# A fused attention and MoE kernel whose matmuls read the moving operand as two interleaved halves

## Chip, core and metric

The kernel runs on one NeuronCore of one Trainium2 chip, as one launch. The metric is the device time of that core in microseconds, taken as the median of three runs; lower is better. No other core works at the same time, and the profile shows the TensorE clock granted at its upper level, 2.4 GHz, through nearly the whole execution.

## What is computed

Four batches of 12480 tokens, 128 channels each, pass through two attentions with 32 inducing points. The 49920 results then pass through one two-layer network with a hidden width of 2048:

```python
h = mab(I, x)                 # 32 x 128 per batch
x = mab(x, h)                 # 12480 x 128 per batch: softmax over 32, times h
h = x @ w_in                  # 49920 x 2048
g = h * (1 / (1 + exp(-1.702 * h)))
out = g @ w_out               # 49920 x 128
```

## The kernel before

**Blocks and chunks.** The output is made in 98 blocks of tokens (list `work`): 96 of 512 tokens, and two of 384 that hold what is left over of two batches each. The hidden width is cut into 16 chunks of 128; two chunks make a step, so a block has 8 steps. Tokens always lie along the free dimension, channels or hidden units on the partitions, so the tokens are the moving operand of every product of the network.

**First products** (`firsts`, L527). A tile `st` holds the stacked softmax weights of a block, 512 tokens wide, and a tile `hw` the 32 rows of h times `w_in` in stacked form. Each chunk is one matmul of 512 columns; the two chunks of a step fill the two PSUM banks of a tile `ph`. There are two `ph` tiles.

**Activation and splitting.** ScalarE applies the activation from `ph` into a float32 tile `g` (`gelus`, L553). From step 12 on, `g` is split into a rounded part `hi` and a rest `lo`: `hi` comes either from ScalarE, a second activation from `ph` (L569), or from VectorE, a copy of `g` (L576), whichever engine `choose` finds less loaded; `lo` is always VectorE's subtraction (L585, `rests`).

**Second products** (`seconds`, L704 to L706). Each chunk adds three matmuls into one PSUM bank `pso`, because `w_out` is split as well: `wl` with `hi`, `wh` with `lo`, `wh` with `hi`. All of these operands are of type fp32r, and a matmul takes one column per clock. The first 24 chunk products (L690) use plain float32 `g` and `wf` instead; each is two matmul instructions, and an instruction takes two clocks per column. The last block is written in `ending` (L627 to L629): its last four chunks are done in halves of 256 columns, the right halves into a second bank `side`, so that most of the result is copied and sent while the right half is still being computed.

**Output.** When a block's 16 chunks are added up, `out` copies `pso` to a tile `ob` on ScalarE (L605) or VectorE (L608), and `store` sends it to `outT`. There are two `pso` banks and two `ob` tiles.

**Attention.** The attentions of batches 1 to 3 are worked in between: TensorE visits of 10 to 35 small matmuls each (L351 and L370 for the first attention, L993 and L359 for the second), with exponentials on ScalarE and transposes, maxima and subtractions on VectorE.

**Order of the work.** The order on each engine is fixed when the program is built. `Plan` is a list scheduler: each `Job` has an engine, an occupation in ns and a latency, and `Plan.step` takes the job that could begin first, by rank among equals. Where a job may go to ScalarE or VectorE, the one that would end first gets it. The occupation of a matmul of `w` columns is one of its costs:

```python
            one_ = 2.5 + 0.447 * tokens(i)
...
                occ = 3 * (2.5 + 0.447 * w)
```

Tiles `st`, `hw`, `hi` and `lo` come from `spaced`, which adds 16 elements to each tile's row; within a tile the 512 tokens of a chunk are one contiguous run of 2 KB per partition.

Of the kernel before, what the change touches and what calls it, by code (L numbers as in the profile page):

```python
# [17 lines left out]
P = 128  # L18
# [252 lines left out]
def on_act(n):  # L271
    return 70 + 0.833 * n, 215 + 0.833 * n


def on_dve(n):
    return 75 + 1.042 * n, 200 + 1.042 * n
# [7 lines left out]
def set_attention_then_moe(ctx: ExitStack, tc, xT, x, indT, w_in, w_out, outT):  # L284
    nc = tc.nc
    dve, act, pe_ = nc.vector, nc.scalar, nc.tensor
# [11 lines left out]
    t0 = 0  # L298
# [65 lines left out]
    def weigh(pa, s, aT, xn, i, n, second=None):  # L364
# [10 lines left out]
            i += 1  # L375
        return i

    def blocks(some):
        return sum(sups[s][2] // 32 for s in some)

    work = []
# [94 lines left out]
    phs, gs, his, los = [[Unit() for _ in range(n)] for _ in range(4)]  # L476
# [6 lines left out]
    def new_st(name):  # L483
        return Unit(NG, parts=G if len(name) == 3 else 2 * RG * G)
# [4 lines left out]
    def tokens(i):  # L489
        return sum(p[2] for p in work[steps[i][0]][1])  # L490

    def late(least, most):
        return lambda: most if ahead() >= AHEAD else least
# [16 lines left out]
    def firsts():  # L510
        for i in range(n):
            bi, k = steps[i]
            key, of = work[bi]
            if key not in st_units:
                st_units[key] = new_st(key)
            for b, _, _, _ in of:
                for c in range(G):
                    h_units.setdefault((b, c), Unit(uses_hw[b], parts=G))
            stu = st_units[key]
            hwu = [h_units[b, 2 * k // 4] for b, _, _, _ in of]  # L520

            def emit(i=i, k=k, of=of, stu=stu, hwu=hwu):
                st, ph = stu.ap, phs[i].ap
                for c in range(2):
                    ch = 2 * k + c
                    for (b, at, w, _), u in zip(of, hwu):
                        pe_.matmul(  # L527
                            ph[:, c, at:at + w], u.ap[:, ch % 4 * P:(ch % 4 + 1) * P],
                            st[:, at:at + w], start=True, stop=True,
                        )  # L530
                counts["F"] = i + 1

            one_ = 2.5 + 0.447 * tokens(i)
            yield Job("PE", emit, 2 * one_, 2 * one_ + 200, [stu, *hwu], takes=[(r_ph, phs[i])], rank=(1, i), slack=late(0, 800),
                gate=lambda: not plan.asked(r_ph),
            )
# [56 lines left out]
    def store(bi, ob):  # L593
        _, of = work[bi]
        for b, at, w, t0 in of:
            def emit(at=at, w=w, t0=t0):
                nc.sync.dma_start(outT[:, t0:t0 + w], ob.ap[:, at:at + w])
            yield Job("SP", emit, 430, 2500, [ob], rank=(3, bi), size=w * 512)

    def out(bi, pso):  # L600
        w = sum(p[2] for p in work[bi][1])
        ob = Unit(len(work[bi][1]))

        def by_act():
            act.copy(ob.ap[:, 0:w], pso.ap[:, 0:w])  # L605

        def by_dve():
            dve.tensor_copy(ob.ap[:, 0:w], pso.ap[:, 0:w])  # L608

        yield [  # L610
            Job("ACT", by_act, *on_act(w), [pso], [], [(r_ob, ob)], rank=(0, bi)),
            Job("DVE", by_dve, *on_dve(w), [pso], [], [(r_ob, ob)], rank=(0, bi)),
        ]
        yield from store(bi, ob)

    def ending(bi, i0):
        w = tokens(i0)
        h = w // 2
        b, at, _, t0 = work[bi][1][0]
        ps, side, kept = Unit(3, parts=NCH), Unit(1, parts=2 * ENDING), Unit(3)  # L620
        firsts_ = [(i, c) for i in range(i0, i0 + NG) for c in range(2)]
        split = firsts_[-2 * ENDING:]

        def three(o, i, c, cols, start, stop):
            ch = 2 * (i - i0) + c
            hi, lo = his[i].ap[:, c, cols], los[i].ap[:, c, cols]
            pe_.matmul(o, wl[:, ch, :], hi, start=start, stop=False)  # L627
            pe_.matmul(o, wh[:, ch, :], lo, start=False, stop=False)  # L628
            pe_.matmul(o, wh[:, ch, :], hi, start=False, stop=stop)  # L629

        def job(i, c, cols, right):
            n_ = cols.stop - cols.start
            first = (i, c) == (split[0] if right else firsts_[0])
            last = (i, c) == firsts_[-1]
            unit = side if right else ps

            def emit():
                three(unit.ap[:, 0:h] if right else unit.ap[:, cols], i, c, cols, first, last)
                counts["S"] += not right

            occ = 3 * (2.5 + 0.447 * n_)
            ch = 2 * (i - i0) + c
            return Job(
                "PE", emit, occ, occ + 200, [his[i], los[i], w_out_units[ch // G]], rank=(2, i),
                **({"takes": [(r_po, unit)]} if first else {"joins": [unit]}),
            )

        for i, c in firsts_:
            his[i].uses += (i, c) in split
            los[i].uses += (i, c) in split  # L650
            yield job(i, c, slice(0, h if (i, c) in split else w), False)

        def keep():
            act.copy(kept.ap[:, 0:w], ps.ap[:, 0:w])

        def add():
            dve.tensor_add(kept.ap[:, h:w], kept.ap[:, h:w], side.ap[:, 0:h])  # L657

        def send(cols):
            def emit():  # L660
                nc.sync.dma_start(outT[:, t0 + cols.start:t0 + cols.stop], kept.ap[:, cols])
            return emit

        done = Unit(1)
        plan.spawn(iter([
            Job("ACT", keep, *on_act(w), [ps], [], [(r_ob, kept)], rank=(0, bi)),
            Job("SP", send(slice(0, h)), 430, 2500, [kept], rank=(3, bi), size=h * 512),
            Job("DVE", add, *on_dve(h), [kept, side], [], joins=[done], rank=(0, bi)),
            Job("SP", send(slice(h, w)), 430, 2500, [done], rank=(3, bi), size=h * 512),
        ]))  # L670
        for i, c in split:
            yield job(i, c, slice(h, w), True)

    def seconds():
        psos = {}
        for i, (bi, k) in enumerate(steps):
            if bi == len(work) - 1:
                yield from ending(bi, i)
                return
            w = tokens(i)  # L680
            if k == 0:
                psos[bi] = Unit(parts=NCH)
            pso = psos[bi]
            for c in range(2):
                ch = 2 * k + c

                join = {"joins": [pso]} if ch else {"takes": [(r_po, pso)]}

                def whole(i=i, c=c, ch=ch, w=w, pso=pso):
                    pe_.matmul(  # L690
                        pso.ap[:, 0:w], wf[:, ch * P:(ch + 1) * P], gs[i].ap[:, c, 0:w],
                        start=(ch == 0), stop=(ch == NCH - 1),
                    )
                    counts["S"] += 1

                if i < plain:
                    occ = 4 * (1 + 0.4185 * w)
                    yield Job("PE", whole, occ, occ + 200, [gs[i], wf_units[ch // G]], rank=(2, i), **join)
                    continue

                def emit(i=i, c=c, ch=ch, w=w, pso=pso):
                    o = pso.ap[:, 0:w]
                    hi, lo = his[i].ap[:, c, 0:w], los[i].ap[:, c, 0:w]
                    pe_.matmul(o, wl[:, ch, :], hi, start=(ch == 0), stop=False)  # L704
                    pe_.matmul(o, wh[:, ch, :], lo, start=False, stop=False)  # L705
                    pe_.matmul(o, wh[:, ch, :], hi, start=False, stop=(ch == NCH - 1))  # L706
                    counts["S"] += 1

                occ = 3 * (2.5 + 0.447 * w)
                yield Job(  # L710
                    "PE", emit, occ, occ + 200, [his[i], los[i], w_out_units[ch // G]], rank=(2, i), **join,
                )
            if k == NG - 1:
                plan.spawn(out(bi, pso))
# [78 lines left out]
    def attention(b):  # L793
# [109 lines left out]
        pah = Unit(parts=len(WEIGH))  # L903
        i = 0
        total = blocks(range(NS))
        for v, some in enumerate(WEIGH):

# [432 lines left out]
    wf = const.tile([P, WHOLE * WC], F32, name="wf") if WHOLE else None  # L1340
# [483 lines left out]
    plan.spawn(fast([2, 3], False))  # L1824
    plan.spawn(to_gelu())
    plan.spawn(firsts())
    plan.spawn(attentions())
    plan.spawn(loads_xT())
# [15 lines left out]
    for thread in (gelus, rests, seconds, lay_out):  # L1844
        plan.spawn(thread())
# [34 lines left out]
```

## Time and profile before

| | us |
|---|---|
| median of 3 runs | 1568.87 |
| lowest, highest | 1568.35, 1569.07 |
| span of the profiled execution, first to last instruction | 1566.2 |
| TensorE (PE) matmul busy | 1559.7 |
| weight loads (PEld) busy | 1226.0 |
| VectorE (DVE) busy | 1340.9 |
| ScalarE (ACT) busy | 1321.2 |

The page gives the span of the profiled execution and no total time for it beside that. The median of the runs is 2.7 us above the span: that is taken here as what lies around it, the start ahead of the first instruction and the wait for the last store.

In the rows, a group is a source line, an engine, an operation, the tile written and the tiles read, the shape and a count; then the busy time in us and the mean duration of one in ns, and behind the second bar the idle time of the engine just before these instructions and what ended it. Matmuls are pipelined: a row's mean duration (393 ns) holds the time in the pipeline, and the pace is the distance from one start to the next.

### The profile page before, as it was taken

Reading aid. Unit: us, or ns where it says so; the run is one execution under the profiler, and the core shown is the slowest. Engines: PE = TensorE matmul, PEld = TensorE weight load, DVE = VectorE, ACT = ScalarE, POOL = GpSimd, SP = SyncE. Lnnn points to the kernel's source line nnn. Section 1 sums busy time; section 2 is a strip of 40 time slices with the busy share of each in tenths; the row PEclk is TensorE's granted clock in tenths of the full one; section 3 lists DMA queues with packets and bytes.
Section 4 is the critical chain, followed back from the end, with each engine's and each line's share of the span. In section 5 each row is a group of like instructions: output and inputs, shape, how many; then the busy total and the mean of one; then the engine's idle time right before and its main releaser. Section 6 shows DMA issues by size and latency. Waiting matters only on the chain. (4 is left out here: it accounts for less than half of the span.)

```text
span 1566.2 us, 21639 instructions
## 1 busy us (share of the span) xinstructions
PE 1559.7 (100%) x7707; PEld 1226.0 (78%) x7707; DVE 1340.9 (86%) x1641; ACT 1321.2 (84%) x1515; POOL 0.7 (0%) x6
## 2 busy tenths in 40 slices
PE   9999999999999999999999999999999999999999
PEld 7477878877877887887787887887788888888887
DVE  6999888888888888889889888988898888888886
ACT  6799888888887888888988888888888888888876
POOL 0000000000000000000000000000000000000000
PEclk9999999999999999999999999999999999999999
DMA  7455144161132404416014512512201111111100
GB/s 272 165 167 141 33 90 91 34 202 48 46 137 86 93 29 95 84 35 220 29 41 151 129 46 53 110 45 84 66 26 46 34 40 33 36 38 31 41 27 21
DMA packets 84617, 125.06 MB, mean 80 GB/s; under 512 B 12128, under 2 KB 51872, under 8 KB 79136
## 3 DMA queue, kind: packets, MB, share of 16 engines
q1 hardware_dynamic: 84512, 123.69, 28.4%
q8 instruction: 62, 1.02, 0.3%
q14 instruction: 43, 0.35, 0.1%
HBM read 70.43 MB, written 25.56 MB: 61 GB/s over the span
## 5 line engine op out<-in xcount | busy, mean ns | idle before, releaser
L585 DVE TENSOR_TENSOR lo<-g,hi 128x1024 fp32r<-128x1024 f32 (+1 forms) x772 | 929.4, 1215 | 164.5 <-ACT hi L569 150.4
L553 ACT ACTIVATE g<-ph 128x1024 f32<-128x1024 f32 (+1 forms) x784 | 805.1, 1032 | 205.7 <-PE ph L527 84.7
L704 PE MATMUL pso<-hi,wl 128*128 128x512 f32 (+1 forms) x1528 | 600.3, 393 | 0.0
L705 PE MATMUL pso<-lo,wh 128*128 128x512 f32 (+1 forms) x1528 | 599.4, 392 | 0.1
L706 PE MATMUL pso<-hi,wh 128*128 128x512 f32 (+1 forms) x1528 | 599.3, 392 | 0.0
L569 ACT ACTIVATE hi<-ph 128x1024 fp32r<-128x1024 f32 (+1 forms) x459 | 473.4, 1033 | 3.8 <-PE pso L706 3.8
L527 PE MATMUL ph<-st,hw 128*128 128x512 f32 x1536 | 457.6, 398 | 0.9 <-ACT g L553 0.9
L527 PEld LDWEIGHTS ph<-st,hw 128*128 128x128 f32 x1536 | 283.0, 188 | 85.2 <-ACT g L553 10.7
L705 PEld LDWEIGHTS pso<-lo,wh 128*128 128x128 f32 x1528 | 287.0, 188 | 66.2 <-DVE lo L585 1.0
L704 PEld LDWEIGHTS pso<-hi,wl 128*128 128x128 f32 x1528 | 287.0, 188 | 65.5 <-issue 0.2
L706 PEld LDWEIGHTS pso<-hi,wh 128*128 128x128 f32 x1528 | 287.0, 188 | 65.2
L576 DVE CAST hi<-g 128x1024 fp32r<-128x1024 f32 (+1 forms) x313 | 211.1, 681 | 27.2 <-ACT g L553 23.4
L605 ACT COPY ob<-pso 128x512 f32<-128x512 f32 (+1 forms) x76 | 45.8, 603 | 6.7 <-PE pso L706 6.7
L690 PE MATMUL pso<-g,wf 128*128 128x512 f32 x48 | 23.2, 598 | 0.1
L351 PE MATMUL pa<-xt,indT_sb 128*32 128x512 f32 x160 | 19.9, 598 | 0.0
L608 DVE COPY ob<-pso 128x512 f32<-128x512 f32 x21 | 14.3, 681 | 4.9 <-PE pso L706 4.8
L370 PEld LDWEIGHTS pa<-xn,t 128*32 128x32 f32 x576 | 15.2, 110 | 3.3 <-issue 2.9
L370 PE MATMUL pa<-xn,t 128*32 128x128 f32 x576 | 17.6, 274 | 0.0
L1133 DVE TENSOR_TENSOR t<-t,two 128x512 f32<-128x512 f32 (+1 forms) x27 | 16.8, 621 | 0.8 <-ACT two L1122 0.2
L1117 DVE STREAM_TRANSPOSE t<-e 128x512 f32<-128x512 f32 x23 | 16.2, 704 | 0.0
L1112 DVE TENSOR_TENSOR e<-e,sm 128x512 f32<-128x512 f32 x23 | 15.6, 680 | 0.0
L1100 DVE TENSOR_REDUCE sm<-e 128x16 f32<-128x512 f32 x23 | 15.6, 678 | 0.0
(203 smaller groups left out, 477.0 us busy)
## 6 DMA issues: line engine op xcount, KB each, us to landing
xt<-in_xT SPq DMA_DIRECT2D x42, 1024.0 KB, 7.1
out_T<-ob SPq DMA_DIRECT2D x95, 256.0 KB, 2.0
xn<-in_x SPq DMA_DIRECT2D x72, 256.0 KB, 6.3
st<-two SPq DMA_DIRECT2D x184, 64.0 KB, 2.0
st<-t SPq DMA_DIRECT2D x184, 64.0 KB, 2.0
hw<-t SPq DMA_DIRECT2D x48, 64.0 KB, 2.8
raw<-in_w_in SPq DMA_DIRECT2D x4, 512.0 KB, 8.7
raw<-in_w_out SPq DMA_DIRECT2D x4, 512.0 KB, 5.0
```

Of the source, the lines that this page charges most:

```text
L351: pe_.matmul(pa[32 * j:32 * j + 32, 0:w], indT_sb, xg[:, j], start=True, stop=True)
L370: pe_.matmul(pa[32 * j:32 * j + 32, 0:P], aT[0:q, kk, :], xn[0:q, kk] if second is None or kk < BLK // 2 else second[0:q, kk - BLK // 2], ...
L527: pe_.matmul(ph[:, c, at:at + w], u.ap[:, ch % 4 * P:(ch % 4 + 1) * P], st[:, at:at + w], start=True, stop=True,)
L553: act.activation(gs[i].ap[:, :, 0:w], phs[i].ap[:, :, 0:w], AF.Gelu_apprx_sigmoid)
L569: act.activation(his[i].ap[:, :, 0:w], phs[i].ap[:, :, 0:w], AF.Gelu_apprx_sigmoid)
L576: dve.tensor_copy(his[i].ap[:, :, 0:w], gs[i].ap[:, :, 0:w])
L585: dve.tensor_sub(los[i].ap[:, :, 0:w], gs[i].ap[:, :, 0:w], his[i].ap[:, :, 0:w].bitcast(F32))
L605: act.copy(ob.ap[:, 0:w], pso.ap[:, 0:w])
L690: pe_.matmul(pso.ap[:, 0:w], wf[:, ch * P:(ch + 1) * P], gs[i].ap[:, c, 0:w], start=(ch == 0), stop=(ch == NCH - 1),)
L704: pe_.matmul(o, wl[:, ch, :], hi, start=(ch == 0), stop=False)
L705: pe_.matmul(o, wh[:, ch, :], lo, start=False, stop=False)
L706: pe_.matmul(o, wh[:, ch, :], hi, start=False, stop=(ch == NCH - 1))
```

## The change

Every matmul of the network reads its moving operand through `woven`: the free dimension is seen as two halves, and columns are taken from the two halves in turns. For a 512-column matmul of 4-byte elements the halves begin 1 KB apart; column 0 is token 0, column 1 token 256, column 2 token 1, and so on. The product's columns in PSUM come out in that order. The activation and the split keep the order they find. The second product weaves once more, so that a block's result has its tokens permuted twice, and the copy from PSUM to `ob` (or, for the last block, `keep`, `add` and `send`) puts them back: it reads PSUM with a step of four elements and writes four runs. The last block's first products are read straight; its second products are woven, and its two stores write runs of 128 tokens to `outT`. In the 384-column blocks the first products weave each batch's 192 columns by themselves. Attention's matmuls are not changed. In the planner the price per column goes from 0.447 to 0.417 ns.

```diff
+    def woven(t):
+        return t.rearrange("p (a b) -> p b a", a=2)
+
+    def unwoven(t, parts):
+        order = "p (c a s) -> p a s c" if parts == 1 else "p (c a s) -> p s a c"
+        return t.rearrange(order, a=2, s=2)
+
+    def runs(t):
+        return t.rearrange("p (s a c) -> p s a c", a=2, s=2)
...
-                            st[:, at:at + w], start=True, stop=True,
+                            order(st[:, at:at + w]), start=True, stop=True,
...
-            one_ = 2.5 + 0.447 * tokens(i)
+            one_ = 2.5 + 0.417 * tokens(i)
...
-            act.copy(ob.ap[:, 0:w], pso.ap[:, 0:w])
+            act.copy(runs(ob.ap[:, 0:w]), unwoven(pso.ap[:, 0:w], len(work[bi][1])))
...
-            dve.tensor_copy(ob.ap[:, 0:w], pso.ap[:, 0:w])
+            dve.tensor_copy(runs(ob.ap[:, 0:w]), unwoven(pso.ap[:, 0:w], len(work[bi][1])))
...
-            hi, lo = his[i].ap[:, c, cols], los[i].ap[:, c, cols]
+            half = slice(cols.start // 2, cols.stop // 2)
+            hi, lo = woven(his[i].ap[:, c, 0:w])[:, half], woven(los[i].ap[:, c, 0:w])[:, half]
...
         def keep():
-            act.copy(kept.ap[:, 0:w], ps.ap[:, 0:w])
+            act.copy(
+                kept.ap[:, 0:w].rearrange("p (q s b) -> p q s b", q=2, s=2),
+                ps.ap[:, 0:w].rearrange("p (q b s) -> p q s b", q=2, s=2),
+            )
 
         def add():
-            dve.tensor_add(kept.ap[:, h:w], kept.ap[:, h:w], side.ap[:, 0:h])
+            right = kept.ap[:, h:w].rearrange("p (s b) -> p s b", s=2)
+            dve.tensor_add(right, right, side.ap[:, 0:h].rearrange("p (b s) -> p s b", s=2))
...
-                nc.sync.dma_start(outT[:, t0 + cols.start:t0 + cols.stop], kept.ap[:, cols])
+                nc.sync.dma_start(
+                    outT[:, t0:t0 + w].rearrange("p (s q b) -> p q s b", q=2, s=2)[:, q],
+                    kept.ap[:, cols].rearrange("p (s b) -> p s b", s=2),
+                )
...
-                    hi, lo = his[i].ap[:, c, 0:w], los[i].ap[:, c, 0:w]
+                    hi, lo = woven(his[i].ap[:, c, 0:w]), woven(los[i].ap[:, c, 0:w])
```

The L690 matmuls and the prices of the second products change in the same way. The number of instructions is the same on TensorE (7021 in the program's order, 7707 in the trace, where a float32 matmul stands more than once) and on SyncE (686). Because of the new price the planner orders them otherwise. On ScalarE the activations into `hi` go from 459 to 471, the copies to `ob` from 76 to 64, the casts L1122 from 17 to 12 and the copies L821 from 14 to 13; on VectorE the casts into `hi` go from 313 to 301, the copies to `ob` from 21 to 33, the casts L1125 from 10 to 15 and the copies L824 from 7 to 8. Lines behind the new helpers are 10 to 20 higher in the changed kernel.

On VectorE, early in the program where batch 1's first attention is being worked in, the order before has one copy of a block's result among the subtractions `lo`:

```order
L585 TENSOR_TENSOR lo<-g,hi 128x1024
L608 COPY ob<-pso 128x512
L1133 TENSOR_TENSOR t<-t,two 128x512
L832 TENSOR_REDUCE mx<-e 128x1
L824 COPY e<-pa 128x512
L832 TENSOR_REDUCE mx<-e 128x1
L576 CAST hi<-g 128x1024
```

and the order of the changed kernel at about the same place:

```order
L595 TENSOR_TENSOR lo<-g,hi 128x1024
L618 COPY ob<-pso 128x512
L595 TENSOR_TENSOR lo<-g,hi 128x1024 x2
L1153 TENSOR_TENSOR t<-t,two 128x512
L586 CAST hi<-g 128x1024 x2
L595 TENSOR_TENSOR lo<-g,hi 128x1024
L852 TENSOR_REDUCE mx<-e 128x1 x2
L852 TENSOR_REDUCE mx<-e_last 64x1
L595 TENSOR_TENSOR lo<-g,hi 128x1024
L586 CAST hi<-g 128x1024
L595 TENSOR_TENSOR lo<-g,hi 128x1024 x4
L618 COPY ob<-pso 128x512
```

The copy of `e` from PSUM and the attention's maxima have moved back behind more subtractions, and the next block's copy has come to VectorE too.

On TensorE, batch 1's second visit of the first attention's products (L370) stands between first and second products of the network. Before:

```order
L704 MATMUL pso<-hi,wl 128x512
L705 MATMUL pso<-lo,wh 128x512
L706 MATMUL pso<-hi,wh 128x512
L370 MATMUL pa<-xn,t 32x128 x32
L527 MATMUL ph<-st,hw 128x512 x4
L704 MATMUL pso<-hi,wl 128x512
```

and in the changed kernel:

```order
L724 MATMUL pso<-hi,wl 128x512
L725 MATMUL pso<-lo,wh 128x512
L726 MATMUL pso<-hi,wh 128x512
L537 MATMUL ph<-st,hw 128x512 x2
L370 MATMUL pa<-xn,t 32x128 x32
L537 MATMUL ph<-st,hw 128x512 x2
```

The visit now splits the two steps of first products, and stands some 50 rows later in TensorE's order (row 720 for row 671).

## Rows read from the trace of the kernel before

**Rows 1.** The page: engines' busy time, share of the span, instructions.
```profile
PE 1559.7 (100%) x7707; PEld 1226.0 (78%) x7707; DVE 1340.9 (86%) x1641; ACT 1321.2 (84%) x1515; POOL 0.7 (0%) x6
```

**Rows 2.** Matmuls by line and shape.
```profile
L704 PE MATMUL pso<-hi,wl 128*128 128x512 f32 x1496 | 589.5, 394 | 0.0
L705 PE MATMUL pso<-lo,wh 128*128 128x512 f32 x1496 | 588.6, 393 | 0.1
L706 PE MATMUL pso<-hi,wh 128*128 128x512 f32 x1496 | 588.5, 393 | 0.0
L527 PE MATMUL ph<-st,hw 128*128 128x512 f32 x1536 | 457.6, 398 | 0.9 <-ACT g L553 0.9
L690 PE MATMUL pso<-g,wf 128*128 128x512 f32 x48 | 23.2, 598 | 0.1
...
L704 PE MATMUL pso<-hi,wl 128*128 128x384 f32 x32 | 10.8, 338 | 0.0
...
L627 PE MATMUL pso<-hi,wl 128*128 128x512 f32 x12 | 4.7, 394 | 0.0
```

**Rows 3.** Timeline, last block: start us, us; 21 starts apart; no DVE, ACT after 1558.61.
```profile
1555.17 0.39 PE L627 MATMUL pso<-hi,wl 128*128 128x512 f32 x1
...
1556.34 1.02 ACT L569 ACTIVATE hi<-ph 128x1024 fp32r<-128x1024 f32 x1
...
1557.39 1.22 DVE L585 TENSOR_TENSOR lo<-g,hi 128x1024 fp32r<-128x1024 f32 x1 [0.59 <-ACT hi L569]
...
1558.65 0.40 PE L627 MATMUL pso<-hi,wl 128*128 128x512 f32 x1
...
1560.04 0.28 PE L627 MATMUL pso<-hi,wl 128*128 128x256 f32 x1
```

**Rows 4.** Timeline of TensorE at 63.5 us: six float32 matmuls in a row.
```profile
63.52 2.74 PE L690 MATMUL pso<-g,wf 128*128 128x512 f32 x6
```

**Rows 5.** Stretches: us, PE, PEld, DVE, ACT, POOL busy (instructions), PEclk, DMA share, GB/s.
```profile
60.00:160.00 100.00, 100.00 (x451) 70.14 (x450) 91.30 (x122) 87.96 (x103) 0.00 (x0) 1.00 0.56 171
760.00:860.00 100.00, 100.00 (x458) 77.40 (x458) 89.36 (x100) 85.06 (x95) 0.00 (x0) 1.00 0.23 78
1260.00:1360.00 100.00, 100.00 (x434) 80.95 (x433) 85.64 (x92) 85.10 (x94) 0.00 (x0) 1.00 0.12 35
```

**Rows 6.** Waits: who waited for whom, us in total, times, longest us.
```profile
DVE lo L585 <- ACT hi L569: 150.4, 236, 1.8
ACT g L553 <- PE ph L527: 84.7, 113, 3.7
...
PEld ph L527 <- ACT g L553: 10.7, 31, 0.8
```

**Rows 7.** Copies of the result, contiguous, and reads with a step beside contiguous ones.
```profile
L605 ACT COPY ob<-pso 128x512 f32<-128x512 f32 x74 | 44.8, 606 | 5.8 <-PE pso L706 5.8
L608 DVE COPY ob<-pso 128x512 f32<-128x512 f32 x21 | 14.3, 681 | 4.9 <-PE pso L706 4.8
...
L1049 ACT ACTIVATE e<-e 128x512 f32<-128x512 f32 x23 | 12.8, 620 | 0.1
L832 DVE TENSOR_REDUCE mx<-e 128x1 f32<-128x512 f32 x18 | 11.9, 675 | 0.1
...
L1288 ACT ACTIVATE sq<-raw 128x512 f32<-128x512 f32 x8 | 5.5, 689 | 0.0
...
L944 DVE TENSOR_REDUCE all_h<-t 32x128 f32<-32x512 f32 x3 | 3.2, 1071 | 0.0
```

**Rows 8.** Timeline of the end.
```profile
1561.64 0.58 ACT L654 COPY ob<-pso 128x512 f32<-128x512 f32 x1 [4.28 <-PE pso L629]
...
1562.25 1.65 SPq L661 DMA_DIRECT2D out_T<-ob  x2
...
1562.74 0.28 PE L629 MATMUL pso<-hi,wh 128*128 128x256 f32 x1
1563.12 0.42 DVE L657 TENSOR_TENSOR ob<-ob,pso 128x256 f32<-128x256 f32 x1 [4.50 <-PE pso L629]
```

More of the change, by code (lines that the diff above doesn't have):

```diff
@@ L520, in firsts, with emit @@
             hwu = [h_units[b, 2 * k // 4] for b, _, _, _ in of]
-            def emit(i=i, k=k, of=of, stu=stu, hwu=hwu):
+            def emit(i=i, k=k, of=of, stu=stu, hwu=hwu, order=woven if bi < len(work) - 1 else lambda t: t):
                 st, ph = stu.ap, phs[i].ap
@@ L639, in emit @@
                 counts["S"] += not right
-            occ = 3 * (2.5 + 0.447 * n_)
+            occ = 3 * (2.5 + 0.417 * n_)
             ch = 2 * (i - i0) + c
@@ L653, in keep @@
         def keep():
-            act.copy(kept.ap[:, 0:w], ps.ap[:, 0:w])
+            act.copy(
+                kept.ap[:, 0:w].rearrange("p (q s b) -> p q s b", q=2, s=2),
+                ps.ap[:, 0:w].rearrange("p (q b s) -> p q s b", q=2, s=2),
+            )
         def add():
-            dve.tensor_add(kept.ap[:, h:w], kept.ap[:, h:w], side.ap[:, 0:h])
+            right = kept.ap[:, h:w].rearrange("p (s b) -> p s b", s=2)
+            dve.tensor_add(right, right, side.ap[:, 0:h].rearrange("p (b s) -> p s b", s=2))
         def send(cols):
+            q = cols.start // h
             def emit():
-                nc.sync.dma_start(outT[:, t0 + cols.start:t0 + cols.stop], kept.ap[:, cols])
+                nc.sync.dma_start(
+                    outT[:, t0:t0 + w].rearrange("p (s q b) -> p q s b", q=2, s=2)[:, q],
+                    kept.ap[:, cols].rearrange("p (s b) -> p s b", s=2),
+                )
             return emit
@@ L690, in whole @@
                     pe_.matmul(
-                        pso.ap[:, 0:w], wf[:, ch * P:(ch + 1) * P], gs[i].ap[:, c, 0:w],
+                        pso.ap[:, 0:w], wf[:, ch * P:(ch + 1) * P], woven(gs[i].ap[:, c, 0:w]),
                         start=(ch == 0), stop=(ch == NCH - 1),
@@ L707, in emit @@
                     counts["S"] += 1
-                occ = 3 * (2.5 + 0.447 * w)
+                occ = 3 * (2.5 + 0.417 * w)
                 yield Job(
```

## Prediction

> **What bounds the kernel now.** I read the page's busy times first, then matmuls by shape, then starts in the timeline, then stretches, waits and copies. The busy times show matmuls for 1559.7 of 1566.2 us, and VectorE and ScalarE at 86% and 84% [rows 1]. Only 6.5 us of TensorE's span are without a matmul, so TensorE's pace sets the end, and a change that leaves that pace alone can hardly help.
>
> A busy share near 100% does not say that the pace is as good as it can be. Nearly all of the span goes to 512-column fp32r matmuls: three lines with 1496 each, 1536 first products and 36 in the last block [rows 2]. Their mean of 394 to 398 ns holds pipeline time, so I take starts. In the last block 21 steps lie between 1555.17 and 1560.04 us: 231.9 ns each [rows 3]. In the stretch from 1260 to 1360 us 434 matmuls show, two of them begun before it: 100 us through 432 is 231.5 ns [rows 5]. The granted clock there is 1.00, the 2.4 GHz level, at which 512 columns are 213.3 ns. About 18 ns in each matmul is neither columns nor a throttled clock.
>
> What takes them? Not the neighbours: ScalarE's last activation ends at 1557.36 and VectorE's last subtraction at 1558.61, and the six steps from 1558.65 to 1560.04 still take 231.7 ns each [rows 3]. Not a fixed price of an instruction either: the 256-column matmuls that follow, 23 steps from 1560.04 [rows 3] to 1562.74 [rows 8], take 117.4 ns against 106.7 for their columns, so most of the loss goes with the columns. And the plain float32 matmuls hardly have it: six in a row last 2.74 us [rows 4]; less one duration of 0.60 [rows 2] and through five that is 428 ns a step, where 1024 clocks (two per column) are 426.7, so some 2 ns are lost per matmul. They read the same kind of contiguous 4-byte words at half the pace. So the loss comes when a new word is wanted on each clock, and it lies on the way of the moving operand in or of the result out.
>
> **The change, part by part.**
>
> *The pace.* Woven, a 512-column matmul alternates between two runs 1 KB apart. No row before shows an fp32r matmul reading so. If the loss comes from taking neighbouring words in a row, what is left is the columns and what the float32 matmuls lose, 213.3 + 2, rounded up to 216 ns. The bounds are 214 (half of the float32 step) and, upward, the case below in which reading in turns costs more. I take 216, since that is columns at the granted clock plus a loss which a row shows. The gain is 231.5 - 216 = 15.5 ns, on 3 x 1496 + 36 + 1520 matmuls (the 16 first products of the last block stay straight): 6044 x 15.5 = 93.7 us. The 96 of 384 columns give three quarters each, 1.1 us; the 24 of 256 columns 0.2; the 192-column ones I put at nothing, as there are 64. Together **95 us**; at 214 ns it would be 107.
>
> The Trainium skill (TensorE: Matmul & The Clock Gate, "Wait — 56ns, not 53.3ns?") gives a start-to-start time of columns over 2.4 GHz plus 2.5 ns for a warm array, 215.7 ns at 512 columns. This trace does not agree for contiguous fp32r operands: 231.5 ns. By the page's figure for the woven ones the gain would be 15.8 x 6044 = 95.5 us, within a microsecond or two of the sum here.
>
> *What hid beside it.* With TensorE's span at 1566.2 - 95 = 1471 us, VectorE's 1341 us become 91% and ScalarE's 1321 become 90%. The reordering adds 2 us to each: VectorE takes 12 copies of 0.68, five casts and a copy of `e` for 12 casts into `hi` given up; ScalarE 12 activations of 1.03 for 12 copies of 0.61 and five casts. Is there a stretch in which that is too much? The densest 100 us have VectorE at 91.3 and 89.4 us [rows 5], while TensorE would need about 93.5 to 94 for the same work. So no long stretch turns over, but short ones will, and six `hi`, six `lo` and two `ph` tiles can level out some 10 us only. At its lowest this costs nothing more. At its highest, VectorE's waits for `hi` from ScalarE, 150.4 us [rows 6], all stay: 1343 + 150 = 1493 us is 22 over TensorE's 1471. What tells of TensorE's own waits for buffers is small, 10.7 us of weight loads waiting for the activation [rows 6]. It is nearer to the lower end; I take **+8 us**.
>
> *The copies.* All 97 read PSUM with a step of 16 bytes and write in four runs. Contiguous they take 606 ns on ScalarE and 681 on VectorE [rows 7]. Reads with a step nearby: ScalarE's square of every second word takes 689 against 620 for a contiguous pass; VectorE's sum across runs 512 bytes apart takes 1071 against 675 for a contiguous reduction [rows 7]. So 0 to 0.40 us more for each; I take 0.07, the plain elementwise row. That is 64 x 0.07 = 4.5 us on ScalarE and 2.3 on VectorE, at most 26 and 13. It lies beside TensorE: there are two `pso` banks, and the next block's 64 matmuls take some 14 us. If that cover is gone the upper end is VectorE's 13 us again, 22 + 13 = 35 in all. A slow copy's queue matters most on VectorE, where more copies now stand between subtractions.
>
> *Moved visits.* Attention's visits keep their matmuls and move by some steps; their cost on TensorE is the same. As many transfers as before are issued, on the one queue, so nothing there.
>
> *The end.* The copy of the left half (0.58 us, ended at 1562.22) may grow by 0.4 and still ends before the last matmul's result. The addition of the right half and the two stores, in rows of half the length, lie on the path: 0.42 and 1.65 us [rows 8]. I take +0.5 us, bounds 0 and 1.5.
>
> *Sum.* 1566.2 - 95 + 8 + 0.5 = 1479.7 us of span; with the 2.7 us by which the median lies above the profiled span, **1482 us**. The forecast's own range is 1568.9 - 107 = 1462 at the best and 1568.9 - 95 + 35 + 1.5 = 1510 at the worst.
>
> **The rivals.**
>
> *The other engines become the bound, or half the loss goes.* TensorE gets its pace, but slow copies on ScalarE (26 us) push `hi` back, and VectorE waits for it on top of the 35 us above: 1510 to 1536 us. A step of 224 ns, the loss halved, gives 1568.9 - 6044 x 0.0075 + 8 = 1532. Together 1510 to 1550. For it: 91% and 90%, with 236 waits for `hi` [rows 6]. Against it: the buffers, and that VectorE and ScalarE now wait for TensorE's products (84.7 us [rows 6]).
>
> *Reading in turns is slower.* Each column comes from another place than the one before, and the operand's read path pays for each change of place. For it: where this kernel reads with a step, it pays, 689/620 = 1.11 and 1071/675 = 1.59 times [rows 7]. Against it: both are other engines, and the price paid now is on contiguous words. At 1.11 the step is 257 ns and the time 1568.9 + 6044 x 0.0255 = 1723 us; at 1.59 it is 368 ns and about 2394; at the float32 pace of two clocks per column, 429 ns, about 2763. It decides from 232 ns on: half a nanosecond per matmul is 3 us.
>
> The Trainium skill (SBUF — State Buffer, "Specifications (TRN2)") speaks against the change in the same sense: memory lines of 16 bytes, at least two hits on a line for full bandwidth, and a penalty for each cross to a new one. No run here shows it for TensorE yet, and by it alone contiguous words should lose nothing, which 231.5 ns contradict.
>
> *The order of reading is not the cause.* The loss lies with the result's way into PSUM, or in the port itself. Both are left alone: 231.5 ns stay, and the time is 1569 to 1572 with the longer end. For it: the trace before has no row that tells the way in from the way out. Against it: first products overwrite PSUM and second ones add to it, and the two have the same kind of duration, 398 and 394 ns [rows 2].
>
> **How the numbers follow.** The forecast has 0.72, the engines or a half gain 0.12, slower reading 0.12, no effect 0.04. The last is what a measurement of this kernel takes for no change, 0.2% or 3 us. So faster 0.84, same 0.04, slower 0.12. The planner's new price of 0.417 moves the order of the work only; it is not counted as evidence of the chip's pace. The range: from 1466, just above the forecast's best, to 1540, which takes in the forecast and about three quarters of the next case, some 0.8.
>
> **What would show it.** Right: starts of 512-column matmuls 215 to 217 ns apart in a stretch without attention, about 464 matmuls in 100 us instead of 434; VectorE and ScalarE at 90% or more; matmul gaps of 10 to 20 us in all; copies of 0.60 to 0.75 us. Wrong: starts at 231 ns with the same engines' shares (no effect), starts over 232 (slower reading), or starts at 216 with TensorE idle for more than 40 us behind the activation or `lo` (the engines).

## The result and the profile after

The changed kernel takes **1496.2 us**, median of four runs, against 1568.84 before: a ratio of 0.9542, 95% interval 0.9528 to 0.9555. It is 72.6 us faster. The forecast was 1482 with a range of 1466 to 1540; the direction, the mechanism and the step of a matmul came out as forecast, and 14 us of the gain did not come.

The page of the changed kernel, span and busy times, answers to [rows 1]:

```profile
span 1494.5 us, 21596 instructions
...
PE 1476.5 (99%) x7707; PEld 1227.6 (82%) x7707; DVE 1334.5 (89%) x1647; ACT 1315.2 (88%) x1509; POOL 0.7 (0%) x6
```

TensorE's matmul time fell by 83.2 us, and its idle time rose from 6.5 us to 18.0. The stretch without attention that stands in [rows 5], now (us, busy time and instructions of PE, PEld, DVE, ACT and POOL, clock, DMA share, GB/s):

```profile
1260.00:1360.00 100.00, 100.00 (x463) 86.51 (x462) 91.04 (x100) 91.63 (x101) 0.00 (x0) 1.00 0.13 38
```

463 matmuls show where 434 did: 100 us through some 461.5 starts is 216.7 ns, in which two or three short waits are included. The last block of the timeline shows the step by itself, as [rows 3] did (start, duration):

```profile
1483.82 0.38 PE L638 MATMUL pso<-hi,wl 128*128 128x512 f32 x1
...
1488.35 0.27 PE L638 MATMUL pso<-hi,wl 128*128 128x256 f32 x1
```

21 steps in 4.53 us are 215.7 ns. Over all 512-column fp32r matmuls of the trace the median distance from start to start is 216 ns where it was 231 to 232.

Groups by line and shape; the matmuls answer to [rows 2], the copies to [rows 7]:

```profile
L724 PE MATMUL pso<-hi,wl 128*128 128x512 f32 x1496 | 568.1, 380 | 0.0
...
L710 PE MATMUL pso<-g,wf 128*128 128x512 f32 x48 | 28.4, 707 | 0.1
L615 ACT COPY ob<-pso 128x512 f32<-128x512 f32 x62 | 38.2, 617 | 3.5 <-PE pso L726 3.2
L618 DVE COPY ob<-pso 128x512 f32<-128x512 f32 x33 | 22.7, 688 | 6.3 <-PE pso L726 5.6 <-DMA hw<-t 0.7
```

and the two activations of the page, 1032 and 1033 ns on the page of before:

```profile
L563 ACT ACTIVATE g<-ph 128x1024 f32<-128x1024 f32 (+1 forms) x784 | 812.9, 1045 | 145.7 <-PE ph L537 68.4
...
L579 ACT ACTIVATE hi<-ph 128x1024 fp32r<-128x1024 f32 (+1 forms) x471 | 494.8, 1053 | 0.6 <-PE pso L726 0.5
```

The copies that read PSUM with a step cost 11 and 7 ns more than contiguous ones. Two rows went the wrong way: the float32 matmuls are longer (707 ns for 598), and so are ScalarE's activations.

In the timeline of TensorE six float32 matmuls in a row, as in [rows 4]:

```profile
66.02 3.40 PE L710 MATMUL pso<-g,wf 128*128 128x512 f32 x6
```

Less one duration of 0.71 us that is 538 ns a step, where it was 428. For the 48 of them this is 5.3 us.

**Where the time went.** The steps give 6044 x 15.5 = 93.7 us and 1 us in the 384-column blocks. The float32 matmuls take 5.3 back. The span fell by 71.7 us, so 17.7 us are left, and these are waits, with a stretch at the lower clock that is shown below: 11.5 us are idle time that shows, and the rest does not show as idle, because a matmul's row holds about 0.16 us of pipeline time beyond its step, which covers short waits. Counted from start to start, the 6060 fp32r matmuls of 512 columns take 12.5 us beyond 231.5 ns each before and 27.5 us beyond 216 ns each now, and attention's L370 visits, behind one of which the longest stand lies, 4.5 us more than before. The waits of the changed kernel (us in total, times, longest), to be held against [rows 6]:

```profile
PEld ph L537 <- ACT g L563: 16.9, 30, 3.4
PEld ph L537 <- ACT hi L579: 15.3, 48, 2.1
...
PE ph L537 <- ACT g L563: 6.6, 13, 3.2
...
PE ph L537 <- ACT hi L579: 3.9, 5, 1.7
```

Between 60 us and the end TensorE's gaps are 12.2 us where they were 1.0, and 11.5 of them lie within 12 us after a load of ScalarE's tables: at the runs of attention's exponentials. The longest is at 222.5 us. ScalarE's timeline there (start, us):

```profile
214.16 1.28 ACT L895 ACT_TABLE_LOAD   x1
...
220.18 1.28 ACT L563 ACT_TABLE_LOAD   x1
221.47 2.85 ACT L563 ACTIVATE g<-ph 128x1024 f32<-128x1024 f32 x3
```

and TensorE's:

```profile
214.73 0.38 PE L724 MATMUL pso<-hi,wl 128*128 128x512 f32 x1
...
216.68 0.38 PE L724 MATMUL pso<-hi,wl 128*128 128x512 f32 x1
...
217.42 1.95 PE L370 MATMUL pa<-xn,t 128*32 128x128 f32 x64
222.55 0.70 PE L537 MATMUL ph<-st,hw 128*128 128x512 f32 x2 [3.18 <-ACT g L563]
223.47 0.86 PE L537 MATMUL ph<-st,hw 128*128 128x512 f32 x2 [0.22 <-ACT g L563]
```

For 7.3 us ScalarE frees no `ph`; TensorE works off its stock of split activations and one visit of attention, and then stands for 3.18 us. The stock is small: the second products of four chunks, two steps, begin in the run, the first at 214.73 and the last at 216.68. The same run before lasted from 204.81 to 212.13. Eight chunks, four steps, began in it, TensorE's stock and visit reached to 213.21, and it lost 0.18 us. The lines of before, of ScalarE and of TensorE:

```profile
204.81 1.28 ACT L875 ACT_TABLE_LOAD   x1
...
205.16 0.39 PE L704 MATMUL pso<-hi,wl 128*128 128x512 f32 x1
...
210.48 0.39 PE L704 MATMUL pso<-hi,wl 128*128 128x512 f32 x1
...
211.26 1.95 PE L370 MATMUL pa<-xn,t 128*32 128x128 f32 x64
...
214.12 0.73 PE L527 MATMUL ph<-st,hw 128*128 128x512 f32 x2 [0.18 <-ACT g L553]
```

Whether the faster pace or the new order of the work left only two steps is settled under "Order or pace". After its stand in the changed kernel the granted clock fell to the lower level, 1.2 GHz (stretches as above):

```profile
222.00:224.00 2.00, 1.23 (x4) 0.81 (x5) 1.44 (x2) 2.00 (x3) 0.00 (x0) 0.97 0.00 0
224.00:226.00 2.00, 2.00 (x6) 1.23 (x6) 2.00 (x4) 1.35 (x2) 0.00 (x0) 0.50 0.42 95
```

6 matmuls show in those last 2 us, where at 216 ns nine would start; the lower level lasted 3.4 us in all.

### The profile page after: what moved, and what is told of

It reads as the page before. It is cut to its first block, busy times and chain, and to the rows that moved or that the text cites. A ratio compares the mean times of both kernels' runs of the same rounds, so it can differ in the third digit from the quotient of the medians.

```text
span 1494.5 us, 21596 instructions
## 1 busy us (share of the span) xinstructions
PE 1476.5 (99%) x7707; PEld 1227.6 (82%) x7707; DVE 1334.5 (89%) x1647; ACT 1315.2 (88%) x1509; POOL 0.7 (0%) x6
## 4 chain that ended last, share of the span: by engine, by line
PE 47%; ACT 2%; DVE 1%; issue 0%; ACTq 0%; DVEq 0%
PE ph L537 12%; PE pso L725 11%; PE pso L724 11%; PE pso L726 11%; ACT g L563 1%; DVE lo L595 1%; ACT hi L579 0%; DVE hi L586 0%; PE pa L370 0%; PE pa L351 0%; PE pso L640 0%; PE pso L638 0%; PE pso L639 0%; ACT e L895 0%; PE ph L359 0%
## 5 line engine op out<-in xcount | busy, mean ns | idle before, releaser
L563 ACT ACTIVATE g<-ph 128x1024 f32<-128x1024 f32 (+1 forms) x784 | 812.9, 1045 | 145.7 <-PE ph L537 68.4
L725 PE MATMUL pso<-lo,wh 128*128 128x512 f32 (+1 forms) x1528 | 578.6, 379 | 1.5 <-DVE lo L595 1.4
L724 PE MATMUL pso<-hi,wl 128*128 128x512 f32 (+1 forms) x1528 | 578.7, 379 | 0.0
L726 PE MATMUL pso<-hi,wh 128*128 128x512 f32 (+1 forms) x1528 | 577.7, 378 | 0.0
L579 ACT ACTIVATE hi<-ph 128x1024 fp32r<-128x1024 f32 (+1 forms) x471 | 494.8, 1053 | 0.6 <-PE pso L726 0.5
L537 PE MATMUL ph<-st,hw 128*128 128x512 f32 x1536 | 452.8, 387 | 10.7 <-ACT g L563 6.6
L586 DVE CAST hi<-g 128x1024 fp32r<-128x1024 f32 (+1 forms) x301 | 202.9, 682 | 17.4 <-ACT g L563 16.9
L615 ACT COPY ob<-pso 128x512 f32<-128x512 f32 (+1 forms) x64 | 39.2, 613 | 3.8 <-PE pso L726 3.6
L618 DVE COPY ob<-pso 128x512 f32<-128x512 f32 x33 | 22.7, 688 | 6.3 <-PE pso L726 5.6
L370 PEld LDWEIGHTS pa<-xn,t 128*32 128x32 f32 x576 | 15.2, 110 | 3.0 <-issue 2.7
L370 PE MATMUL pa<-xn,t 128*32 128x128 f32 x576 | 17.6, 274 | 0.0
L710 PEld LDWEIGHTS pso<-g,wf 128*128 128x128 f32 x48 | 8.9, 190 | 10.0 <-issue 8.4
```

The source lines that it names most:

```text
L370: pe_.matmul(pa[32 * j:32 * j + 32, 0:P], aT[0:q, kk, :], xn[0:q, kk] if second is None or kk < BLK // 2 else second[0:q, kk - BLK // 2], ...
L537: pe_.matmul(ph[:, c, at:at + w], u.ap[:, ch % 4 * P:(ch % 4 + 1) * P], order(st[:, at:at + w]), start=True, stop=True,)
L563: act.activation(gs[i].ap[:, :, 0:w], phs[i].ap[:, :, 0:w], AF.Gelu_apprx_sigmoid)
L579: act.activation(his[i].ap[:, :, 0:w], phs[i].ap[:, :, 0:w], AF.Gelu_apprx_sigmoid)
L586: dve.tensor_copy(his[i].ap[:, :, 0:w], gs[i].ap[:, :, 0:w])
L615: act.copy(runs(ob.ap[:, 0:w]), unwoven(pso.ap[:, 0:w], len(work[bi][1])))
```

## Experiments

**What way of reading costs what.** A kernel of nothing but streams of matmuls, each stream with another access pattern.

```diff
+    for i in range(TIMES):
+        pe_.matmul(o[i % 2], w, m5, start=True, stop=True)                 # L52
...
+        pe_.matmul(o[i % 2], w, turns(m5, 2), start=True, stop=True)       # L55
+        pe_.matmul(o[i % 2], w, turns(m5, 4), start=True, stop=True)       # L58
...
+        pe_.matmul(o[i % 2], w, near(m5, 64), start=True, stop=True)       # L73
```

> Nothing of the network is computed: 40 matmuls of 512 columns for each of 22 ways of reading the moving operand, back to back, with no other engine at work; the output holds one copied product again and again. Theory (the loss comes from taking neighbouring 4-byte words of fp32r one after the other): contiguous 231 ns from start to start, in the first stream and the last; two halves 1 KB apart 216; any other reading in turns of places far apart (four quarters, sixteen parts, halves 2 KB apart) 216 as well; runs of two or more words from each half between 216 and 231. Rival (the distance of 1 KB matters): 216 for 1 KB, 231 or more for the others. Rival (weight loads beside the stream take the time): contiguous with 32 stationary columns in place of 128 falls to 216. Float32, from the changed kernel: contiguous 429 ns, two halves in turns 540; if that is a price for every change of place, runs of two words lie near 485 and every 16 bytes is at 540 too. bf16 contiguous: 216.

The timeline of TensorE, one row for a stream (start, length of the whole stream, matmuls). A step is the length less one matmul's duration, through 39, or 79 for float32, where a matmul is two instructions:

```profile
18.40 9.23 PE L52 MATMUL o<-m,w 128*128 128x512 f32 x40
27.47 8.80 PE L55 MATMUL o<-m,w 128*128 128x512 f32 x40
36.10 11.49 PE L58 MATMUL o<-m,w 128*128 128x512 f32 x40
...
64.80 18.64 PE L64 MATMUL o<-m,w 128*128 128x512 f32 x40
...
109.96 8.80 PE L73 MATMUL o<-m,w 128*128 128x512 f32 x40
...
168.90 9.43 PE L91 MATMUL o<-m,w 128*32 128x512 f32 x40
178.18 8.81 PE L94 MATMUL o<-mb,wb 128*128 128x512 bf16 x40
186.82 19.54 PE L97 MATMUL o<-mb,wb 128*128 128x512 bf16 x40
...
240.53 43.36 PE L103 MATMUL o<-x 128*128 128x512 f32 x80
```

| moving operand, 512 columns | step, ns |
|---|---|
| fp32r, contiguous (L52) | 227 |
| fp32r, two halves in turns: 1 KB (L55), 2 KB, 64 B or 16 B apart (L73) | 216 |
| fp32r, four quarters in turns (L58) | 283 |
| fp32r, sixteen parts in turns | 434 |
| fp32r, every 16 B (L64); every 8 B | 461; 452 |
| fp32r, runs of two, four, sixteen words from two halves | 333, 250, 240 |
| fp32r, one word for all columns | 219 |
| fp32r, contiguous, 32 stationary columns (L91) | 232 |
| bf16, contiguous (L94); two halves in turns (L97) | 216; 484 |
| float32, contiguous; two halves (L103) | 429; 540 |
| float32, runs of two from two halves; every 16 B | 453; 900 |

All three readings were wrong in part. That contiguous fp32r words cost time and two halves don't is borne out. But turns among more than two places are slower, not equal; the 1 KB is of no importance, 16 B do as well; and lighter weight loads do not take the loss away, since with a quarter of the stationary columns the contiguous step is 232. What pays is narrow: single 4-byte words from just two places in turns, each place read in order. For bf16 and float32 the same pattern costs time, and for float32 there is no one price for a change of place: runs of two take 453, not 485, and every 16 B 900, not 540. Why two places in turns suit fp32r words is not shown by these streams.

The Trainium skill (SBUF — State Buffer, "Specifications (TRN2)") asks for two hits on a line of 16 bytes and names a penalty for each cross to a new one. By that rule every 16 B and sixteen parts must be slow, and they are (461, 434); halves 16 B apart must lose as well against contiguous words, and they gain (216 against 227). Every 8 B and runs of two have two words on a line, so by the rule they may pass, and they take 452 and 333. So the rule holds for a part of this table only, and not for the row that this change lives on.

**Order or pace.** The new planner price alone, on contiguous reading, and the woven reading with the old price.

```diff
-            one_ = 2.5 + 0.447 * tokens(i)
+            one_ = 2.5 + 0.417 * tokens(i)
```

> The kernel before with the planner's new price of 0.417 ns per column alone; every operand is read contiguously. Theory (the way of reading makes the gain, the price only orders the work): 512-column steps of 231.5 ns and a time of 1565 to 1575 us. Rival (the new order of the work makes a good part of the gain): 1530 us or less.

> The changed kernel with the planner's old price of 0.447. Theory: steps of 216 ns stay; the order is laid out for a slower TensorE, so its waits differ by some us: 1490 to 1508 us. Rival (order): 1530 us or more.

| | contiguous | woven |
|---|---|---|
| price 0.447 | 1568.6 | 1505.3 |
| price 0.417 | 1576.6 | 1496.2 |

The price alone makes the kernel 8.0 us slower (ratio 1.0049, 1.0033 to 1.0066), a little more than the theory's upper end: an order laid out for a faster TensorE than there is. The woven reading alone makes it 63.3 us faster, and the price that fits it 9.1 more. So the gain is the reading's, and a planner's price is worth about half a per cent either way.

The same two runs tell where the long stand comes from. With the price alone, at 231.5 ns a matmul, TensorE stands for 2.93 us behind the run of exponentials that costs it 3.18 in the changed kernel:

```profile
218.46 1.28 ACT L875 ACT_TABLE_LOAD   x1
...
226.85 0.73 PE L527 MATMUL ph<-st,hw 128*128 128x512 f32 x2 [2.93 <-ACT g L553]
```

With the woven reading and the old price, at 216 ns, it stands for 0.66 us:

```profile
204.20 1.28 ACT L895 ACT_TABLE_LOAD   x1
...
212.58 0.70 PE L537 MATMUL ph<-st,hw 128*128 128x512 f32 x2 [0.66 <-ACT g L563]
```

| price, reading | chunks of second products begun in this run | stand behind it, us | TensorE's gaps from 60 us on, us | time of 512-column matmuls beyond 231.5 or 216 ns each, us |
|---|---|---|---|---|
| old, contiguous | 8 | 0.18 | 1.0 | 12.5 |
| new, contiguous | 4 | 2.93 | 6.9 | 17.5 |
| old, woven | 8 | 0.66 | 10.1 | 38.4 |
| new, woven | 4 | 3.18 | 12.2 | 27.5 |

The stock at the start of a run follows the order and not the pace. Counted as `hi` tiles made less steps begun, over the runs from 100 us on, it is 3.5 to 5.5 steps with the old price, in either way of reading, and 2 to 4.5 (once 6) with the new. The planner asks for 5 steps by its own count before such a run, unless the first products have already reached a mark; why the chip had fewer was not looked at. So the long stands belong to the order that the new price makes, and the faster pace by itself brings many short waits, which that order shortens again by 11 us.

**The float32 matmuls read straight.**

```diff
+    def again(bi, t):
+        return woven(t) if bi > 1 else t
...
-                        pso.ap[:, 0:w], wf[:, ch * P:(ch + 1) * P], woven(gs[i].ap[:, c, 0:w]),
+                        pso.ap[:, 0:w], wf[:, ch * P:(ch + 1) * P], gs[i].ap[:, c, 0:w],
...
-                    hi, lo = woven(his[i].ap[:, c, 0:w]), woven(los[i].ap[:, c, 0:w])
+                    hi, lo = again(bi, his[i].ap[:, c, 0:w]), again(bi, los[i].ap[:, c, 0:w])
```

> The changed kernel, with the second products of blocks 0 and 1 (the 48 float32 matmuls among them) read straight and the copy of these two blocks put in order accordingly; the planner's order is the same. Theory (float32 matmuls lose 111 ns each by reading in turns): their steps go from 540 back to 429 ns, 48 x 0.111 = 5.3 us less, the 48 fp32r matmuls of these blocks lose 48 x 0.0155 = 0.7 us: 1491 to 1493 us. Rival (the loss there is hidden, since the opening is bound by other work): 1495 to 1497 us.

1492.94 us (0.9520, 0.9506 to 0.9534): 3.3 us less than the changed kernel, within what was expected; 5.3 us less the 0.7 that contiguous fp32r words cost in these two blocks would be 4.6. The six in a row are back to [rows 4]:

```profile
64.24 2.74 PE L718 MATMUL pso<-g,wf 128*128 128x512 f32 x6
```

In the profiled execution, the slowest of the four (1495.16 us), the clock stood at its lower level for 10.2 us instead of 3.4, behind two of TensorE's stands at runs of exponentials. Whether that is what keeps the median short of the 4.6 us is not shown.

**Why 231.5 in the kernel and 227 in the stream.**

```diff
+        pe_.matmul(o[i % 2], w, m[:, 2:514], start=True, stop=True)                          # L59
...
+        pe_.matmul(o[i % 2], w, (m5, m[:, 1040:1552])[i % 2], start=True, stop=True)         # L74
...
+        pe_.matmul(o[i % 2], w, turns(m[:, 4:516], 2), start=True, stop=True)                # L80
```

> Nothing of the network is computed: streams of 40 matmuls again, and three streams beside which ScalarE copies two PSUM banks eight times. Contiguous streams showed 227 ns alone and 231.5 in the kernel before. Theory (the start address of the operand, or its alternation, makes the 4 ns): one of the shifted or alternating contiguous streams shows 229 to 238, and halves in turns 216 in every form. Rival (it is the kernel's other work): all contiguous streams show 227. Eight parts in turns: between the 283 of four and the 434 of sixteen. bf16 in runs of two from two halves: if two places at a time are what a matmul likes, near 216 and not the 484 of single elements. ScalarE's copies of 1024 columns: if a faster TensorE makes its reads of PSUM longer, they take 10 to 30 ns more beside halves in turns than beside contiguous reads; otherwise they are equal.

Streams as above, the first with the same pattern as L52:

```profile
18.63 9.23 PE L56 MATMUL o<-m,w 128*128 128x512 f32 x40
27.70 9.51 PE L59 MATMUL o<-m,w 128*128 128x512 f32 x40
...
73.73 9.41 PE L74 MATMUL o<-m,w 128*128 128x512 f32 x40
...
92.21 8.80 PE L80 MATMUL o<-m,w 128*128 128x512 f32 x40
...
118.11 19.67 PE L89 MATMUL o<-m,w 128*128 128x512 f32 x40
```

Begun at word 2 the contiguous step is 234 ns (L59), and with two operands in turns it is 231, spread from 225 to 241 (L74): the kernel's own mean and spread. Alone, the two operands of L74 take 227 and 229. So the loss of contiguous words depends on where they begin and on what was read before; that this is what makes the kernel's 231.5 fits, but was not followed matmul by matmul. Halves in turns take 216 from word 4 (L80) as from word 0. Eight parts in turns take 487 (L89), above the range given. bf16 in runs of two from two halves takes 272, in runs of eight (16 bytes) 216. ScalarE's copies of 1024 columns took 1012 ns beside halves in turns and 1015 beside contiguous reading, so TensorE's reading does not make them longer.

**The stock at the runs of exponentials.** Four kernels on top of the straight float32; first, begin a run only with 5.5 steps in stock.

```diff
-LUMP = 5
+LUMP = 5.5
```

> The kernel with float32 read straight, and the run of exponentials on ScalarE begun only when the stock of split activations is 5.5 steps instead of 5 (a constant of the planner). Theory (TensorE's new waits are the runs of exponentials, through which its stock of six steps does not last): half a step more is 0.65 us more cover for each run, so the waits fall by 3 to 6 us: 1487 to 1491 us. Rival (ScalarE and VectorE are too full at 88 to 89% everywhere): 1492 to 1497 us.

1491.15 us (0.9506, 0.9491 to 0.9520), 1.8 less, at the upper end expected, with all four runs below the lowest of the four without it; TensorE's gaps went from 12.1 to 10.4 us and the one of 3.18 us stayed, with four chunks begun in its run as before.

Then each first attention's run in two, at least eight steps apart:

```diff
-                gate=lambda: ahead() >= LUMP or counts["F"] >= i0 + 80, table="exp",
+                gate=lambda: (
+                    (ahead() >= LUMP or counts["F"] >= i0 + 80)
+                    and (not later or 0 < begun[0] <= counts["F"] - later)
+                ), table="exp",
...
-        plan.spawn(exponentials(list(range(4, NS))))
+        plan.spawn(exponentials(list(range(4, NS)), 8))
```

> The kernel with float32 read straight, and the seven exponentials of each batch's first attention done in two runs at least eight steps apart instead of one run of 8.4 us; this loads ScalarE's tables three times more (six loads of 1.28 us, 7.7 us more work on ScalarE). Theory (the runs are the waits): the longest waits, 3.2, 1.7 and 1.3 us, go, and with the first of them the stretch at half the granted clock: 1484 to 1489 us in spite of ScalarE's added work. Rival (too full everywhere): ScalarE's added work makes it 1495 to 1501 us.

1503.24 us (0.9582, 0.9566 to 0.9598), 10 slower: the rival's number or a little worse. The longest gap, at 219 us, fell to 1.4 us and a second of 1.1 came behind it, gaps of 1.7 to 2.6 us stand at other runs, and the sum went to 18.2. My reading, that the runs' length is the matter, falls. The added table loads are 7.7 us of ScalarE's time; that they make the 10 us is not shown, since the order of the work changed with them.

Then, on top of 5.5 steps, the second attention's two runs in one:

```diff
-            yield from second(b, visits, [order[0:4], order[4:]], (pw_, products))
+            yield from second(b, visits, [order], (pw_, products))
```

> The kernel with float32 read straight and the stock of 5.5 steps, and the exponentials of each later batch's second attention in one run of seven instead of two runs of four and three: three runs fewer in all, and 7.7 us less of table loads on ScalarE. Theory after the split (each run costs TensorE a wait of about a microsecond, longer runs cost little more): three waits fewer and less work, 1485 to 1490 us. Rival (the length of a run is what empties the stock): the three longer runs of 8 us cost 1 to 3 us more each, 1493 to 1499 us.

1498.42 us, 7.3 slower than with two runs: the merged runs have gaps of 2.6, 2.3 and 0.8 us behind them. Neither fewer nor shorter runs are better.

And, also on top of 5.5 steps, with the planner's mark for other work raised:

```diff
-AHEAD = 4
+AHEAD = 5
```

> The kernel with float32 read straight and the stock of 5.5 steps, and the planner's mark for doing other work at all (attention's on VectorE, and first products put off) raised from a stock of 4 steps to 5. Theory (what counts is the stock when a run begins): it is as full as the mark of 5.5 made it, so little changes: 1488 to 1493 us. Rival (the stock is drained by VectorE's attention work as well): some waits outside the runs go, but these are under 1 us in all, so under 1490 is not to be had.

1492.24 us, 1.1 more than without. Gaps behind the runs went from 10.0 to 6.5 us: the run of batch 1's first attention now begins at 237.75 us, the second products of ten chunks begin in it, and no stand follows. Yet the time did not follow, for the waits too short to show as gaps grew: what the 512-column matmuls take beyond 216 ns each went from 25.8 to 29.7 us.

**How full the engines are.** The changed kernel without the subtraction for `lo`; the products with `lo` read `hi`, so the result leaves out the rest:

```diff
-                dve.tensor_sub(
-                    los[i].ap[:, :, 0:w], gs[i].ap[:, :, 0:w], his[i].ap[:, :, 0:w].bitcast(F32)
-                )
...
-                    hi, lo = woven(his[i].ap[:, c, 0:w]), woven(los[i].ap[:, c, 0:w])
+                    hi, lo = woven(his[i].ap[:, c, 0:w]), woven(his[i].ap[:, c, 0:w])
```

> The changed kernel without the subtraction that makes lo: the matmuls of wh with lo read hi instead, so the rest of the activations is left out of the result; TensorE's matmuls are the same in number, shape and way of reading, and the planner orders the lighter work anew. VectorE's 923 us of subtractions go. Theory (waits come from the load of the two engines, which the shorter steps no longer cover): with both engines far from full TensorE's waits fall to a few us, and the time is that of its steps, 1478 to 1484 us. Rival (the stock of six steps cannot cover a run of exponentials, however free the engines are otherwise): the waits behind the runs stay and the time is 1490 us or more. ScalarE's activations from PSUM: if VectorE's work beside them is what made them 13 to 20 ns longer in the changed kernel, they fall back to 1033 ns or below.

1481.06 us in one run. The page:

```profile
PE 1467.1 (99%) x7707; PEld 1233.9 (83%) x7707; DVE 736.1 (50%) x1300; ACT 990.7 (67%) x1090; POOL 0.7 (0%) x6
...
L563 ACT ACTIVATE g<-ph 128x1024 f32<-128x1024 f32 (+1 forms) x784 | 794.6, 1022 | 420.6 <-DVE hi L586 287.3
```

Gaps within 12 us behind a table load are 1.0 us, though there are more such loads than before (32 for 26): with engines at 50% and 67% the stock is fuller when a run begins, 5 steps of `hi` or more in eleven of the thirteen runs from 100 us on. The 512-column matmuls take 12.8 us beyond 216 ns each, as little as before the change (12.5 beyond 231.5). Three stands of 1.65 us remain where VectorE waits for the products of attention's L370 visits, 5.9 us of gaps in all. That is the theory's number. The order is another one here as well, so the run shows what the waits cost and not what each cause has in them. The activations take 1022 ns where they took 1045. VectorE's work beside them is lighter here, but so is ScalarE's own mix, so which of the two does it stays open.

## Why the prediction was right, and where it was off

*What bounds the kernel* was right: 231.5 ns, not columns, not clock, not neighbours. That contiguous words are the cause was the bet of the forecast, and the streams bear it out. The reason given was too general, though: "taking neighbouring words in a row" would let any reading in turns help, and would have forecast the same 216 ns for four quarters, which take 283. That the change has two places and no more is luck as far as this reason goes.

*The pace* was right to 0.3 ns: 216 forecast, 215.7 to 216 measured, 95 us in the sum and 94.7 worked out from the trace. The Trainium skill's figure (TensorE: Matmul & The Clock Gate, "Wait — 56ns, not 53.3ns?"), 215.7 ns, is that of the woven fp32r matmuls here, and of contiguous bf16 ones (216); for contiguous fp32r operands no run shows it (227 to 234).

*The float32 matmuls* are the step that was left out. The sum gave the 48 woven L690 instructions no term, although the argument had just shown that they lose hardly anything as they were, so there was nothing to win and an unknown to bound. They cost 5.3 us. Here the rival "reading in turns is slower" holds: 1.26 times.

*What hid beside it* was mis-sized: +8 us against 17.7 measured, within the 0 to 35 of the text. The nearest row was taken to be the 10.7 us of weight loads waiting for an activation. That row belongs to the order before, and the order that the new price makes was given 2 us of work on each engine and no waits. It has them at the old pace too: the price alone raised TensorE's gaps from 1.0 to 6.9 us. The row that bears on it is a stretch: a run of exponentials of 7.3 us against the stock at its start. One step has six second products: 6 x 231.5 = 1.39 us, at 216 ns 1.30. Four steps and a visit outlasted the run by a microsecond before and fall 0.66 us short of it at 216 ns; the two steps of the new order fall 2.93 us short at the old pace and 3.18 at the new. The text had said that six `hi` and six `lo` level out "some 10 us only", and did not lay the runs beside it; six steps were not in stock at either.

*The copies* at 0 to 0.40 us more came out at 0.01, near the lower end, and *the end* at 0.1 us: from the last matmul's start to the end of the span it is 3.59 us where it was 3.47. The median lies 1.8 us above the profiled span, not 2.7. So of the 14 us the float32 matmuls are 5.3 and the waits 9.7, and these last two take 1.3 off.

*The rivals.* The engines as the new bound came about in part (17.7 us of waits, of which the new order has its share; 1481 us with VectorE and ScalarE relieved), not to the 1510 of that case. No effect and slower reading fell for fp32r.

The best version that the runs gave is the changed kernel with float32 read straight and 5.5 steps in stock: 1491.15 us, its interval of 0.9491 to 0.9520 below the changed kernel's 0.9528 to 0.9555.

## What to carry to other kernels

Work out the step of a stream from starts and hold it against columns over the granted clock: a TensorE that is busy for 99.6% of the time lost 7% inside each matmul. Before an access pattern is changed everywhere, measure it once for each type and number of passes in a kernel of streams alone; here the same pattern gains 5% for fp32r, costs 26% for float32 and 124% for bf16. And when the bounding engine gets faster, lay each long stretch in which its suppliers do something else beside the stock that must last through it: count that stock in the trace, where it was two steps, and not in tiles, of which there are six. Where a new order comes with the change, run the order alone as well; here it had the long stand at the old pace.

## What was not expected of the hardware

- Two places in turns are the only reading of fp32r words here that takes 216 ns; one word for all columns takes 219, contiguous words 227 to 234 by the first word and by what is read around them, more than two places 283 to 487.
- Even 16 bytes between the two places are enough (216 ns), so the turns need no other part of the memory.
- bf16 is the reverse: contiguous 216, two halves in turns 484, runs of 16 bytes from two halves 216.
- Activations from PSUM took 13 to 20 ns longer in the changed kernel (1045 and 1053 for 1032 and 1033); TensorE's way of reading beside a copy alone does not do it (1012 for 1015). The cause is open.
